# Seven scale-and-shift operations by VectorE instead of ScalarE, in three norms, and a new order of issue

## The chip, the cores and the metric

The kernel runs on one core of one Trainium2 chip. A core has TensorE (PE, matmuls into PSUM), VectorE (DVE), ScalarE (ACT), GpSimd (POOL) and SyncE (SP, which issues nearly all transfers). Each engine takes its own instructions strictly in the order in which they were written for it, and waits at an instruction until what it needs is there. The metric is device microseconds (us) of one execution; of several runs the median counts.

## The reference

One transformer block over a sequence of 2048 rows of width 512, conditioned on a vector `c`:

```
mod = silu(c) @ w_mod                      # six vectors: sa, ca, ga, sb, cb, gb
h = layernorm(x) * (1 + ca) + sa           # first norm, scale and shift
x = x + ga * (attention(h) @ wo)           # 32 heads of 16, each row sees 8 rows, 2 apart
h = layernorm(x) * (1 + cb) + sb           # second norm, scale and shift
x = x + gb * ((gelu(h @ w_gate) * (h @ w_up)) @ w_down)     # width 1792
```

The scale `1 + ca` and shift `sa` are one number for each of the 512 columns. After the norm the tile is transposed, so that a column lies in one partition; scale and shift are then one instruction on 128 partitions with a scalar for each partition.

## The kernel before

The sequence is cut into four groups (0 to 3; the "third group" is group 2) of 512 rows. Each group passes through the same steps:

- first norm `LN1.g`: statistics and normalizing on VectorE and ScalarE, one power on GpSimd, a transposition by DMA (`LN1.g.t`; for groups 0 and 1 by TensorE), and four scale-and-shift operations, one for each 128 columns (`h0` to `h3`, `transp_ev`, lines 511 to 530);
- twelve projections `qp.g.blk.j` (query, key, value; line 632), each four matmuls into one of four PSUM buffers called `mm`, emptied by ScalarE (lines 648 to 652);
- attention: products of query and key by VectorE (`pq`, line 710), their sums over a head by TensorE (`LTp`, line 727), the softmax (maximum, difference, exponential on ScalarE at line 755, sum, reciprocal, product at lines 744 to 775), a round trip of the weights through DRAM (lines 802 and 809), products with the values by VectorE (`pv`, lines 821 and 886), sums by TensorE (lines 837 and 907), emptied by ScalarE into `oT` (lines 848 and 920), output projection (line 930), and its sum with `x` by VectorE (line 939);
- second norm `LN2.g`, as the first; for group 0 in two halves of 256 rows (`half_ev`, lines 957 to 974), which makes eight scale-and-shift operations of half the size;
- the feed-forward part: 14 pairs of gate and up projections (`g`, `u`, line 991; the first two pairs of group 0 in halves, line 1004), gelu and a cast on ScalarE (lines 1038 and 1045), their product on VectorE (`hht`, line 1056), and four down projections (`y`, line 1018), added to `x` on VectorE (line 1063) and stored.

What stands behind what on each engine is set by the table `ORDER` at the top of the file. Every step is a thread of operations (`Op`), and `ORDER` lists 923 thread numbers: `Issuer.run` takes the next operation of that thread and writes its instructions. An operation also names what it takes and gives back (a PSUM buffer, a tile); the table's order decides which buffer it gets and whom it must wait for. So attention of later groups runs between feed-forward matmuls of earlier ones.

Which engine does a scale-and-shift operation is set by two constants: `DVE_H` (line 489, by norm: which of `h0` to `h3` go to VectorE; empty before) and `HALF_DVE` (line 955, for group 0's second norm: pairs of half and column block). The two engines do the same arithmetic with other instructions:

```
nc.vector.tensor_scalar(out=o, in0=o, scalar1=sc(dt), scalar2=bi(dt), op0=ALU.mult, op1=ALU.add)
nc.scalar.activation(out=o, in_=..., func=ACT.Identity, scale=sc(dt), bias=bi(dt))
```

Of the kernel before, what the change touches and what calls it, by code (L numbers as in the profile page):

```python
# [15 lines left out]
NEG = -4.0e9  # L16

ORDER = [
# [37 lines left out]
]  # L56


# [49 lines left out]
def kernel(  # L108
# [377 lines left out]

    PART = ((0, (0, 1), False), (0, (2, 3), True), (1, (0,), False), (1, (1, 2, 3), True))

    DVE_H = {}

    BY_PE = ("LN1.1",)

# [14 lines left out]
    def transp_ev(key, dkey, dtag, sc, bi, ev, dep, eng=False):  # L507
        pe = ev in BY_PE
        for dtp in range(2):
            for dd in range(2):  # L510
                dt = 2 * dtp + dd

                onv = dt in DVE_H.get(ev, ())
                if onv != eng:
# [437 lines left out]
            yield Op("SP", 0.9, f, after=[f"LN2.0.x{2 * h + 1}"], take=[] if h else [SL["h2"]], give=[SL["xn"]] if h else [],  # L952
                     fire=f"LN2.0.th{h}", lat=0.6)

    HALF_DVE = ((1, 2), (1, 3))

    def half_ev(eng):
        for h in range(2):
            for dt in range(DT):
                if ((h, dt) in HALF_DVE) != eng:  # L960
                    continue
# [188 lines left out]
```

## Time and profile before

| | |
|---|---|
| median of 3 runs | 237.56 us (235.99 to 239.63) |
| the profiled execution | 236.0 us, of which the span from first to last instruction is 234.3 us |
| VectorE busy | 183.6 us (78%), 262 instructions |
| ScalarE busy | 148.7 us (63%), 279 instructions |
| GpSimd busy | 16.2 us (7%) |
| granted TensorE clock | 1.00 over the whole span |
| read from and written to HBM | 21.47 MB and 5.57 MB |

How to read the profile's rows. In the timeline a row is: start in us, length in us, engine, line, operation, output <- input, shapes, and the number of instructions merged into it; in brackets how long the engine had idled before, and who released it. Instructions of one engine overlap a little (the next starts before the last one's write-back has ended), so the time that one costs in a row of equal ones is the distance between starts. This matters most for TensorE, whose single matmul is shown with 0.38 us although the next starts 0.216 us later. In the table by stretches, a row is: stretch in us, its length, and for each engine the busy time and instructions, then granted clock, DMA share and GB/s. In the chain of waits a row is start, length, engine, what.

### The profile page before, as it was taken

What the parts mean: (1) busy time and instruction counts of PE and PEld (TensorE: products, weight loads), DVE (VectorE), ACT (ScalarE), POOL (GpSimd) and SP (SyncE); (2) the same over time, 40 slices, a digit from 0 to 9 for tenths busy, and PEclk for the clock granted to TensorE, in tenths of its full rate; (3) what the DMA queues carried; (4) which work ended last, traced back from release to release, by engine and by line L of the source; (5) the groups of instructions that cost most, each with busy time, mean ns of one, the idle gap of its engine ahead of it and who ended that gap; (6) DMA issues with size and microseconds to landing.
All of it is one profiled execution on the core that took longest, in us unless ns stands there. A gap on an engine that the chain in (4) does not pass through costs nothing.

```text
span 234.3 us, 3756 instructions
## 1 busy us (share of the span) xinstructions
PE 228.3 (97%) x1408; PEld 111.2 (47%) x1408; DVE 183.6 (78%) x262; ACT 148.7 (63%) x279; POOL 16.2 (7%) x38
## 2 busy tenths in 40 slices
PE   7999999999989999999999999999999999999995
PEld 2897444454554434444444344444444444444443
DVE  4699989999999999999999698999996831222222
ACT  6699997697897557955769544463764126666400
POOL 3212320121200000010000001000000100000000
PEclk9999999999999999999999999999999999999999
DMA  6998779939658795016700223131111060000021
GB/s 221 358 351 233 222 233 296 277 118 375 135 155 275 217 345 187 1 46 162 223 3 1 61 65 60 30 90 45 25 46 67 0 134 25 0 0 0 3 67 45
DMA packets 37769, 30.43 MB, mean 130 GB/s; under 512 B 22520, under 2 KB 34296, under 8 KB 37752
## 3 DMA queue, kind: packets, MB, share of 16 engines
q1 hardware_dynamic: 37216, 29.68, 43.3%
q10 hardware_dynamic: 536, 0.53, 0.6%
q8 instruction: 11, 0.18, 0.3%
q14 instruction: 6, 0.05, 0.1%
HBM read 21.47 MB, written 5.57 MB: 115 GB/s over the span
## 4 chain that ended last, share of the span: by engine, by line
PE 79%; ACT 14%; DMA 5%; ACTq 0%; issue 0%; SPq 0%; DVE 0%
PE g_ps L991 20%; PE u_ps L991 20%; PE y_ps L1018 19%; PE qkv_ps L632 7%; PE x_ps L930 6%; DMA x<-in_A_x_dram 3%; PE LTp L727 3%; ACT hT L524 2%; DMA wm<-in_w_mod_dram 2%; PE o_ps L907 2%; ACT gl L412 2%; ACT gl L406 1%; PE y_ps L1029 1%; ACT h L969 1%; ACT kT L650 1%; ACT qT L648 1%
## 5 line engine op out<-in xcount | busy, mean ns | idle before, releaser
L991 PE MATMUL g_ps<-h,Wg 128*128 128x512 bf16 x216 | 55.5, 379 | 0.1
L991 PE MATMUL u_ps<-h,Wu 128*128 128x512 bf16 x216 | 55.4, 379 | 0.0
L1038 ACT ACTIVATE gl<-g_ps 128x512 bf16<-128x512 f32 x56 | 33.8, 604 | 21.0 <-PE g_ps L991 19.9
L1018 PE MATMUL y_ps<-Wd,hht 128*128 128x512 bf16 x210 | 46.1, 379 | 0.0
L1045 ACT CAST ub<-u_ps 128x512 bf16<-128x512 f32 x56 | 33.0, 589 | 18.9 <-PE u_ps L991 18.9
L1056 DVE TENSOR_TENSOR hht<-gl,ub 128x512 bf16<-128x512 bf16 x56 | 22.8, 417 | 21.7 <-ACT ub L1045 21.6
L710 DVE TENSOR_TENSOR pq<-qT,kT 128x4096 bf16<-128x4096 bf16 (+1 forms) x17 | 36.2, 2152 | 0.0
L632 PE MATMUL qkv_ps<-hT,wqkv 128*128 128x512 bf16 x144 | 32.9, 380 | 0.7 <-ACT hT L524 0.6
L991 PEld LDWEIGHTS <-Wg 128*128 128x128 bf16 x216 | 20.9, 98 | 26.3 <-issue 1.9
L991 PEld LDWEIGHTS <-Wu 128*128 128x128 bf16 x216 | 20.8, 98 | 26.3 <-issue 1.3
L1018 PEld LDWEIGHTS <-hht 128*128 128x128 bf16 x210 | 20.5, 98 | 24.8
L632 PEld LDWEIGHTS <-wqkv 128*128 128x128 bf16 x144 | 15.8, 114 | 16.7 <-issue 3.6
L1063 DVE TENSOR_TENSOR ot<-y_ps,x 128x512 bf16<-128x512 f32 x15 | 10.2, 686 | 13.0 <-PE y_ps L1018 13.0
L454 POOL TENSOR_TENSOR rstd<-rstd,neghalf 128x4 f32<-128x4 f32 (+1 forms) x10 | 9.3, 932 | 149.3 <-DVE rstd L443 81.7
L524 ACT ACTIVATE h<-h,modT,scl 128x512 bf16<-128x512 bf16 x12 | 8.8, 803 | 16.9 <-DMA h<-xn 11.9
L886 DVE TENSOR_TENSOR pv<-PT,V 128x4096 bf16<-128x4096 bf16 x8 | 18.1, 2282 | 0.4 <-PE LTp L727 0.4
L930 PE MATMUL x_ps<-woP,oT 128*128 128x512 bf16 x64 | 15.5, 380 | 0.3 <-ACT oT L920 0.2
L423 DVE BATCH_NORM_STATS2 st<-x 128x6 f32<-128x512 bf16 x19 | 12.4, 675 | 2.5 <-DMA x<-in_A_x_dram 2.5
L939 DVE TENSOR_TENSOR x<-x_ps,x 128x512 bf16<-128x512 f32 x16 | 10.7, 680 | 2.7 <-PE x_ps L930 2.6
L571 PE MATMUL qkv_ps<-hT,wqkv 128*128 128x256 bf16 x96 | 11.3, 273 | 0.0
L571 PEld LDWEIGHTS <-wqkv 128*128 128x128 bf16 x96 | 10.3, 113 | 0.7 <-issue 0.6
L930 PEld LDWEIGHTS <-oT 128*128 128x128 bf16 x64 | 6.0, 98 | 8.3 <-ACT oT L920 1.0
(97 smaller groups left out, 234.8 us busy)
## 6 DMA issues: line engine op xcount, KB each, us to landing
V<-vscr SPq DMA_DIRECT2D x12, 526.0 KB, 5.4
wm<-in_w_mod_dram SPq DMA_DIRECT2D x4, 512.0 KB, 7.5
out_dram<-ot SPq DMA_DIRECT2D x15, 128.0 KB, 1.9
Wg<-in_B_w_gate_dram SPq DMA_DIRECT2D x4, 448.0 KB, 4.7
Wu<-in_B_w_up_dram SPq DMA_DIRECT2D x4, 448.0 KB, 6.8
vscr<-vT SPq DMA_DIRECT2D x3, 528.0 KB, 4.5
x<-in_A_x_dram SPq DMA_DIRECT2D x3, 512.0 KB, 8.7
Wd<-in_B_w_down_dram SPq DMA_DIRECT2D x3, 512.0 KB, 6.2
```

Source lines behind the costliest of these rows:

```text
L423: nc.vector.bn_stats(out=k["st", c4][:], in_=src()[:, c4, :])
L524: nc.scalar.activation(out=o, in_=B[key, dtp][:, :, dd, :] if pe else o, func=ACT.Identity, scale=sc(dt), bias=bi(dt))
L571: nc.tensor.matmul(B["qu", h, blk, u][:, jj, :], lhsT=wqkv[blk][:, dt, 2 * u + jj::4], rhs=B["hT", 0][:, 2 * h:2 * h + 2, dt, :], start=st ...
L632: nc.tensor.matmul(ps[:], lhsT=wqkv[blk][:, dt, j::4], rhs=B["hT", sg][:, :, dt, :], start=(dt == 0), stop=(dt == DT - 1))
L710: nc.vector.tensor_tensor(out=B["pq", sg, j][:, :, c0:c1], in0=_ap(B["qT", sg][:, j, c0:c1], [[0, W], [1, c1 - c0]]), in1=_ap(kT[:, j, sg ...
L886: nc.vector.tensor_tensor(out=t[:], in0=_ap(B["PT", sg][:, 0, :], [[SG, 2], [0, 4], [1, SG]]), in1=_ap(v[:, j, 0, :], [[8, 2], [VR, 4], [1 ...
L930: nc.tensor.matmul(ps[:], lhsT=B["oT", sg][:, j, c4 * P:(c4 + 1) * P], rhs=woP[:, j, :], start=(j == 0), stop=(j == 3))
L991: nc.tensor.matmul(ps[:], lhsT=Wt[:, dt, ft * P:(ft + 1) * P], rhs=B["h2T", sg][:, :, dt, :], start=(dt == 0), stop=(dt == DT - 1))
L1018: nc.tensor.matmul(ps[:], lhsT=B["hh", sg, ft][:, c4 * P:(c4 + 1) * P], rhs=B["Wd", ft // 4][:, ft % 4, :], start=(ft == 0), stop=(ft == F ...
L1038: nc.scalar.activation(out=gl[:], in_=B["g", sg, ft][:], func=ACT.Gelu_apprx_tanh)
L1045: nc.scalar.copy(out=ub[:], in_=B["u", sg, ft][:])
L1056: nc.vector.tensor_tensor(out=hh[:], in0=B["gl", sg, ft][:], in1=B["ub", sg, ft][:], op=ALU.mult)
```

## The change

It does three things.

1. `DVE_H` gives `h1` and `h3` of the third group's first norm and of group 3's second norm to VectorE, two of four each.
2. `HALF_DVE` gives VectorE, of group 0's second norm, five of eight: blocks 2 and 3 of the first half and 1, 2 and 3 of the second. Two of them it had before.
3. `ORDER` is another list of the same length.

No operation is added or removed: ScalarE has seven fewer, VectorE seven more, and TensorE, GpSimd and SyncE have the same ones in another order.

```
-    0, 29, 29, 29, 2, 3, 39, 39, 39, 40, 39, 0, 1, 29, 1, 29, 29, 29, 29, 17, 17, 29, 29, 29, 29, 45, 29, 18, 29,
+    29, 29, 29, 29, 0, 2, 39, 39, 39, 1, 39, 29, 29, 29, 29, 29, 3, 1, 39, 40, 17, 17, 40, 17, 37, 40, 0, 45, 29,
...
-    DVE_H = {}
+    DVE_H = {"LN1.2": (1, 3), "LN2.3": (1, 3)}
...
-    HALF_DVE = ((1, 2), (1, 3))
+    HALF_DVE = ((0, 2), (0, 3), (1, 1), (1, 2), (1, 3))
```

The places on which the prediction rests, in the program's own order. In these rows a name ends in a buffer number; the numbers differ between the two programs.

ScalarE at the third group's first norm, before. `L755` is group 0's exponential, `L412` a square with its sum for group 3's norm, `L648` to `L652` empty a projection out of PSUM, `L524` are the scale-and-shift operations:

```order
L652 CAST vO_592<-qkv_ps_621 128x512
L412 ACTIVATE gl_645,sums_568<-x_387,sums_568 128x512
L755 ACTIVATE LTp_455<-LTp_455 128x1024
L652 CAST vO_592<-qkv_ps_650 128x512
L648 CAST qT_594<-qkv_ps_656 128x512
L650 CAST kT_137<-qkv_ps_661 128x512
L648 CAST qT_594<-qkv_ps_666 128x512
L524 ACTIVATE hT_679<-hT_679,modT_128,scl_129 128x4x128 x4
L650 CAST kT_137<-qkv_ps_686 128x512
```

And after:

```order
L652 CAST vO_609<-qkv_ps_629 128x512
L755 ACTIVATE LTp_452<-LTp_452 128x1024
L412 ACTIVATE gl_663,sums_613<-x_552,sums_613 128x512
L648 CAST qT_619<-qkv_ps_643 128x512
L650 CAST kT_137<-qkv_ps_655 128x512
L524 ACTIVATE hT_634<-hT_634,modT_128,scl_129 128x4x128
L648 CAST qT_619<-qkv_ps_695 128x512
L524 ACTIVATE hT_634<-hT_634,modT_128,scl_129 128x4x128
L650 CAST kT_137<-qkv_ps_701 128x512
```

Two of the four `L524` are gone; one emptying that stood ahead of the four now stands between the two that are left, and the exponential has moved ahead of a square and behind one emptying of the value projection.

VectorE at the same place, before. `L760` to `L775` end group 0's softmax, `L463` normalizes rows for group 3's first norm, `L710` are group 1's query-key products, `L821` the first value products of group 0:

```order
L760 TENSOR_REDUCE ssum_675<-LTp_455 128x128
L766 RECIPROCAL rinv_677<-ssum_675 128x128
L463 TENSOR_SCALAR xn_698<-x_387,mv_567,rstd_569 128x512
L775 TENSOR_TENSOR e_712<-LTp_455,rinv_677 128x2x4x128
L463 TENSOR_SCALAR xn_698<-x_387,sums_568,rstd_569 128x512 x2
L710 TENSOR_TENSOR pq_748<-qT_594,kT_137 128x4096
L710 TENSOR_TENSOR pq_777<-qT_594,kT_137 128x4096
L463 TENSOR_SCALAR xn_698<-x_387,sums_568,rstd_569 128x512
L710 TENSOR_TENSOR pq_805<-qT_594,kT_137 128x4096
L821 TENSOR_TENSOR pv_808<-PT_745,V4_714 128x2048 x2
```

And after, where `L522` are the scale-and-shift operations:

```order
L522 TENSOR_SCALAR hT_634<-hT_634,scl_129,modT_128 128x4x128
L766 RECIPROCAL rinv_669<-ssum_665 128x128
L522 TENSOR_SCALAR hT_634<-hT_634,scl_129,modT_128 128x4x128
L775 TENSOR_TENSOR e_674<-LTp_452,rinv_669 128x2x4x128
L710 TENSOR_TENSOR pq_676<-qT_619,kT_137 128x4096
L463 TENSOR_SCALAR xn_689<-x_552,mv_612,rstd_614 128x512
L710 TENSOR_TENSOR pq_746<-qT_619,kT_137 128x4096
L710 TENSOR_TENSOR pq_748<-qT_619,kT_137 128x4096
L463 TENSOR_SCALAR xn_689<-x_552,sums_613,rstd_614 128x512 x3
L821 TENSOR_TENSOR pv_808<-PT_691,V4_678 128x2048 x2
```

Both moved operations stand ahead of `L775`, whose result goes to DRAM and back before `L821` can start; group 3's normalizing now ends behind the third `L710` instead of ahead of it.

VectorE at group 0's second norm, before. `L966` are its scale-and-shift operations, the softmax is group 1's, `L710` are group 2's products:

```order
L710 TENSOR_TENSOR pq_1096<-qT_710,kT_137 128x4096
L760 TENSOR_REDUCE ssum_1098<-LTp_779 128x128
L966 TENSOR_SCALAR h2_1085<-h2_1085,scl_129,modT_128 128x2x128 x2
L766 RECIPROCAL rinv_1124<-ssum_1098 128x128
L775 TENSOR_TENSOR e_1126<-LTp_779,rinv_1124 128x2x4x128
L710 TENSOR_TENSOR pq_1140<-qT_710,kT_137 128x4096
```

And after:

```order
L710 TENSOR_TENSOR pq_1088<-qT_729,kT_137 128x4096
L966 TENSOR_SCALAR h2_1104<-h2_1104,scl_129,modT_128 128x2x128 x2
L760 TENSOR_REDUCE ssum_1119<-LTp_793 128x128
L966 TENSOR_SCALAR h2_1104<-h2_1104,scl_129,modT_128 128x2x128 x3
L766 RECIPROCAL rinv_1126<-ssum_1119 128x128
L775 TENSOR_TENSOR e_1128<-LTp_793,rinv_1126 128x2x4x128
L710 TENSOR_TENSOR pq_1138<-qT_729,kT_137 128x4096
```

The first half's two stand ahead of the sum, the second half's three behind it, all ahead of the reciprocal. Further down, on TensorE, one group of four `u` matmuls (the up projection of block 10 in group 1) that stood behind the first two output projections of group 2 (`L930`, eight matmuls) now stands ahead of them, directly behind the attention sums `L907` from which ScalarE makes their input; and group 2's gate projection of block 13 stands ahead of group 3's first two output projections instead of behind them.

Among the transfers, group 3's input `x3` is issued behind three weight transfers instead of ahead of them, and the transposition `LN1.3.t` stands at the same place of the queue, but waits for normalizing that VectorE now does later.

72 rows, old and new, of the table ORDER are left out of this document.

## Prediction

> **What bounds the kernel now.** I read the page first, then the busy time by stretches, then TensorE's timeline for gaps, then ScalarE's and VectorE's rows beside each gap.
>
> ```profile
> PE 228.3 (97%) x1408; PEld 111.2 (47%) x1408; DVE 183.6 (78%) x262; ACT 148.7 (63%) x279; POOL 16.2 (7%) x38
> 30.00:36.00 6.00, 5.32 (x23) 2.38 (x22) 5.42 (x10) 6.00 (x11) 1.48 (x3) 1.00 0.74 245
> 60.00:66.00 6.00, 5.50 (x28) 2.78 (x27) 6.00 (x12) 5.45 (x11) 1.24 (x3) 1.00 0.63 120
> 72.00:98.00 26.00, 26.00 (x182) 11.25 (x181) 25.30 (x28) 17.39 (x38) 0.00 (x0) 1.00 0.66 214
> 98.00:126.00 28.00, 27.98 (x164) 11.88 (x163) 27.43 (x30) 19.48 (x30) 1.03 (x1) 1.00 0.34 91
> ```
>
> The columns after the length are PE, weight loads, DVE, ACT, POOL. TensorE is full but for a few places, and the busy shares understate the gaps there, because an isolated matmul is shown longer than it costs in a row. VectorE is as full as TensorE up to 126 us: what it takes over has no idle time to fall into.
>
> ```profile
> 183.01 12.09 PE y_ps L1018 x56
> 25.98 8.59 PE L632 MATMUL qkv_ps<-hT,wqkv 128*128 128x512 bf16 x38
> 36.07 7.07 PE qkv_ps L632 x32
> 64.46 0.60 PE L1004 MATMUL g_ps<-h,Wg 128*128 128x256 bf16 x2
> 69.62 1.02 PE L991 MATMUL g_ps<-h,Wg 128*128 128x512 bf16 x4
> 131.87 1.05 PE L907 MATMUL o_ps<-pv,Mph 128*32 128x512 bf16 x16
> 132.85 0.61 PE L930 MATMUL x_ps<-woP,oT 128*128 128x512 bf16 x2
> 135.19 1.03 PE L991 MATMUL u_ps<-h,Wu 128*128 128x512 bf16 x4
> ```
>
> The rate is 12.09 / 56 = 0.216 us for a matmul of 512 columns, so 0.865 for a group of four. *Gap A:* nine groups of group 1's projections start at 25.98 and could be done at 25.98 + 36 x 0.216 = 33.76, group 2's first at 34.62; its second starts at 36.07, 1.45 late. *Gap B:* 32 half-size matmuls (0.108 each, 3.46) lie between 64.46 and 69.62, which is 5.16: 1.70 lost. *Gap C:* eight output projections (1.73) take from 132.85 to 135.19: 0.61 lost. All three together are 3.8 us. No edit of this kind can bring more.
>
> ```profile
> 28.90 0.86 ACT L412 ACTIVATE gl<-x,sums 128x512 bf16<-128x512 bf16 x1
> 29.61 1.15 ACT L755 ACTIVATE LTp<-LTp 128x1024 f32<-128x1024 f32 x1
> 31.98 0.75 ACT L648 CAST qT<-qkv_ps 128x512 bf16<-128x512 f32 x1
> 32.46 3.08 ACT L524 ACTIVATE hT<-hT,modT,scl 128x512 bf16<-128x512 bf16 x4
> 35.30 0.72 ACT L650 CAST kT<-qkv_ps 128x512 bf16<-128x512 f32 x1
> 63.65 2.07 ACT L969 ACTIVATE h<-h,modT,scl 128x256 bf16<-128x256 bf16 x4
> 66.57 1.09 ACT L969 ACTIVATE h<-h,modT,scl 128x256 bf16<-128x256 bf16 x2
> 67.68 1.28 ACT L1038 ACT_TABLE_LOAD   x1
> 132.97 1.07 ACT L920 CAST oT<-o_ps 128x512 bf16<-128x512 f32 x2 [2.89 <-PE o_ps L907]
> ```
>
> Gap A ends with the four scale-and-shift operations and the emptying behind them, gap B with ScalarE's six, the table load and the first gelu, gap C with the emptying of the attention sums. ScalarE ends every gap.
>
> **The change part by part.**
>
> *Third group's first norm.* One operation costs ScalarE (35.30 - 32.46) / 4 = 0.71, one emptying 32.46 - 31.98 = 0.48. With one emptying moved behind `h0`, ScalarE starts `h0` at 31.98, then empties until 33.17, does `h2` until 33.88, and has emptied the buffer that group 2's second projection waits for at 34.36. TensorE is ready at 34.62. Gap A closes: a lead of 1.45, if VectorE's two come in time.
>
> ```profile
> 25.24 0.73 DVE L463 TENSOR_SCALAR xn<-x,mv,rstd 128x512 bf16<-128x512 bf16 x2
> 25.89 0.40 DVE L463 TENSOR_SCALAR xn<-x,sums,rstd 128x512 bf16<-128x512 bf16 x1
> 30.79 1.22 DVE L760 TENSOR_REDUCE ssum<-LTp 128x128 f32<-128x1024 f32 x1 [0.51 <-ACT LTp L755]
> 34.28 0.73 DVE L463 TENSOR_SCALAR xn<-x,sums,rstd 128x512 bf16<-128x512 bf16 x2
> 34.39 0.33 SPq L802 DMA_DIRECT2D escr<-e  x1
> 42.27 4.63 DVE L821 TENSOR_TENSOR pv<-PT,V 128x2048 bf16<-128x2048 bf16 x4 [0.34 <-DMA PT<-escr]
> 62.25 2.28 DVE L710 TENSOR_TENSOR pq<-qT,kT 128x4096 bf16<-128x4096 bf16 x1
> 64.45 1.21 DVE L760 TENSOR_REDUCE ssum<-LTp 128x128 f32<-128x1024 f32 x1
> 65.58 0.59 DVE L966 TENSOR_SCALAR h<-h,scl,modT 128x256 bf16<-128x256 bf16 x2
> 66.09 0.94 DVE L766 RECIPROCAL rinv<-ssum 128x128 f32<-128x128 f32 x1
> 68.21 2.28 DVE L710 TENSOR_TENSOR pq<-qT,kT 128x4096 bf16<-128x4096 bf16 x1
> 128.95 2.28 DVE L886 TENSOR_TENSOR pv<-PT,V 128x4096 bf16<-128x4096 bf16 x1
> ```
>
> The new full-size operation has no row. Nearest is `L463`, same engine operation and shape: (25.89 - 25.24) / 2 = 0.33. The tile is strided in blocks of 128, as `L966`'s is, whose half costs (66.09 - 65.58) / 2 = 0.26; twice that, 0.51, is the upper end. I take 0.33, since `L966` pays a start for each half. What it delays: the exponential comes 0.71 - 0.48 = 0.23 earlier (a square behind it, an emptying ahead), one normalizing of 0.33 leaves, two operations of 0.33 enter, a short `rstd` of 0.1 moves ahead. The weights are done 34.28 - 0.23 - 0.33 + 0.66 + 0.1 = 34.48 to, without the overlap that the moved normalizing had, 34.6: 0.2 to 0.3 later, and with them the store at 34.39. VectorE waited 0.34 for their return before 42.27. Its queue fills that: three products of 64.45 - 62.25 = 2.20 and four normalizings from 34.55 on give 42.5. So the value products start at 42.55, 0.3 late by either road. The lead of 1.45 is mostly gone there: TensorE waits for these products and for the scaling of `wo` behind them, and 0.3 late on VectorE means TensorE can keep only what it had spare.
>
> *Group 0's second norm.* From 42 to 66 VectorE has no idle time and the same instructions in another order, so the products at 62.25 start at 62.55 and end at 64.75. Two halves at 0.26 end at 65.27, the sum (65.58 - 64.45 = 1.13) at 66.40, three halves at 67.18. ScalarE starts its first at 64.0 (its forerunner, the exponential, follows VectorE's 0.3), does two of 0.50 each, two emptyings, the third at 66.45, and then the table load: 67.7 instead of 68.96. The first gelu empties its buffer at 68.3. TensorE's last input, `h3`, comes at 67.2, and after it three half groups of 0.43 remain: 68.6. So the row at 69.62 comes at about 68.7: lead 0.9. Gap B shrinks from 1.7 to about 0.8, now ended by VectorE.
>
> *VectorE behind it.* The products at 68.21 start at 68.21 + 0.3 + 3 x 0.26 = 69.3, 1.1 late. Between 72 and 126 VectorE idles 0.70 + 0.57 = 1.27, all of it waiting for others; late, it waits less. So the last value product of group 2, at 128.95, starts between 128.8 (all absorbed) and 130.05 (none) and ends 2.2 later, at 131.0 to 132.25. TensorE comes to these sums at 131.87 - 0.9 = 130.97, to the second eight of them at 131.4. I take near full absorption, because the waits in question are short and at TensorE's pace.
>
> *Gap C.* An up-projection group of 0.865 now stands between the attention sums and the output projection, while ScalarE's two emptyings (1.07) run; the last of them is needed only by the fourth matmul, 0.65 later still. Gain 0.6. This cover holds as long as the last product is on time; else TensorE waits at the sums.
>
> *At no price:* group 3's second norm. The old operations run inside 12.09 us of down projections:
>
> ```profile
> 191.60 2.93 ACT L524 ACTIVATE h<-h,modT,scl 128x512 bf16<-128x512 bf16 x4 [7.92 <-DMA h<-xn]
> 48.59 2.94 ACT L524 ACTIVATE hT<-hT,modT,scl 128x512 bf16<-128x512 bf16 x4
> 39.80 3.71 SPq L483 DMA_TRANSPOSE hT<-xn  x1
> hT<-xn SPq DMA_TRANSPOSE x2, 4.3
> ```
>
> They end at 194.53, before 195.10. Two on VectorE end earlier, but the output projection moved 0.865 closer uses that up; were the cover gone, each microsecond would cost one. `x3`, later by three transfers, is hidden by the work that stands ahead of its first reading on ScalarE. The start (a warm-up matmul moved out of an idle stretch, dummy exponentials elsewhere) I put at 0.1 lost, bounds 0 to 0.3, from one matmul of 0.216 and a short activation.
>
> [...] The row says 0.33 for the moved operation. [...]
>
> **Sum.** Lead 0.9, gap C 0.6, start -0.1: 1.4 us off the profiled execution's 236.0, so 234.6. The median shown is 1.56 above that execution; with the same distance, 236.2.
>
> **The rivals.**
>
> *VectorE keeps it all.* Nothing of its lag is absorbed: the last product ends at 132.25, TensorE's lead there falls from 0.9 to 0.1 (its second eight started at 132.36), gap C still closes: gain 0.6, 237.0. For it: 25.30 of 26.00 busy. Against it: the idle time is there.
>
> *GpSimd blocks the moved operations.* In the new order the power for group 3's norm is released directly ahead of `h1`.
>
> ```profile
> 5.97 1.52 POOL L454 TENSOR_TENSOR rstd<-rstd,neghalf 128x2 f32<-128x2 f32 x2 [3.32 <-DVE mv L429]
> 6.72 0.73 DVE L463 TENSOR_SCALAR xn<-x,mv,rstd 128x512 bf16<-128x512 bf16 x2
> ```
>
> If it held VectorE for its 0.76, everything from 42.55 on would be later by that: gain 0.5 to 0.6, 237.0. The row against it: beside the second power VectorE's two took 0.73, as at 25.24. [...]
>
> *Slower: the transposition for group 3.* Its rows are now normalized at 42.5, not 39.7, so it is issued 2.8 later. ScalarE wants it at about 48.05, half a microsecond before the old 48.59, since the emptyings ahead of it come that much earlier. Landing in 4.3 leaves 1.2. Beyond 5.5 after issue TensorE waits one for one, since the whole of group 3's projections queue behind; at 6.9 the gain is gone, at 8 it is 1 us slower, 238.7. For it: its issue alone took 3.71 in this crowded stretch. Against: both landed in 4.3.
>
> *More.* If the weights return early and VectorE is not late at all, up to 1 us more of the lead survives: 235.2; all three gaps closed would be 233.8.
>
> **Chances.** Forecast 0.52, VectorE keeps it 0.2, GpSimd 0.05, transposition 0.1, more 0.08, unnamed 0.05. The range 233.8 to 238.7 runs from all gaps closed to the transposition's case. A measurement can tell about 2% (4.75 us) from no change; no case but an unnamed one reaches that: faster 0.04, within 0.91, slower 0.05.
>
> **What would show it.** Step one: no gap around 34 to 36 us, and the chain there without `L524`. Step two: `L821` starts at 42.3 to 42.8 and TensorE waits before the first `L930`. Step three: full-size `g` matmuls at 68.7, VectorE's products at 69.3. Step four: no idle before the second `L930` group near 132. VectorE rows of line 522 well over 0.4, `L821` after 43.5, or `L524` waiting for a transfer near 48 would make it wrong.

## The result and the profile after

The changed kernel takes 235.5 us (median of 20 runs, 234.33 to 238.77), the one before 237.59 (20 runs beside it). The ratio is 0.9918, with a 95% interval of 0.9891 to 0.9945: 0.8% faster, 1.95 us, which is less than the 2% that count as a difference here. The ratio and its interval are formed from the fast executions alone, the medians from all. The forecast was 236.2, in a range of 233.8 to 238.7. The profiled execution took 234.34 us, its span is 232.5.

The page's busy line and the table by stretches of the changed kernel, with the columns as before:

```profile
PE 226.4 (97%) x1397; PEld 111.3 (48%) x1408; DVE 185.1 (80%) x269; ACT 144.6 (62%) x272; POOL 18.2 (8%) x38
...
30.00:36.00 6.00, 6.00 (x30) 3.13 (x28) 5.57 (x9) 5.40 (x11) 1.46 (x3) 1.00 0.82 262
60.00:66.00 6.00, 5.77 (x33) 3.21 (x31) 6.00 (x12) 5.52 (x12) 1.12 (x3) 1.00 0.59 120
72.00:98.00 26.00, 25.95 (x181) 11.11 (x180) 26.00 (x29) 18.01 (x40) 0.00 (x0) 1.00 0.57 171
98.00:126.00 28.00, 27.93 (x164) 12.16 (x164) 27.72 (x31) 19.41 (x29) 1.03 (x1) 1.00 0.39 110
```

Between 30 and 36 us TensorE went from 5.32 to 6.00 of 6.00: gap A is gone. VectorE went from 25.30 to 26.00 in 72 to 98 and from 27.43 to 27.72 in 98 to 126: of its 1.27 us of idle time in these stretches 0.99 is gone. TensorE's rows at the three gaps (a row's count can be one short, where a matmul's record is missing):

```profile
26.18 17.47 PE L632 MATMUL qkv_ps<-hT,wqkv 128*128 128x512 bf16 x80
...
48.21 1.89 PE L930 MATMUL x_ps<-woP,oT 128*128 128x512 bf16 x7 [0.73 <-ACT kT L650]
...
64.39 0.27 PE L1004 MATMUL g_ps<-h,Wg 128*128 128x256 bf16 x1
...
64.88 0.52 PE L1004 MATMUL g_ps<-h,Wg 128*128 128x256 bf16 x3 [0.22 <-ACT h L969]
...
68.44 1.03 PE L991 MATMUL g_ps<-h,Wg 128*128 128x512 bf16 x4
...
130.62 1.05 PE L907 MATMUL o_ps<-pv,Mph 128*32 128x512 bf16 x16
131.60 1.04 PE L991 MATMUL u_ps<-h,Wu 128*128 128x512 bf16 x4
132.47 1.89 PE L930 MATMUL x_ps<-woP,oT 128*128 128x512 bf16 x7
...
226.40 3.22 PE L1029 MATMUL y_ps<-Wd,hht 128*128 128x384 bf16 x28
```

Eighty projection matmuls now run in one row from 26.18. The 32 half-size matmuls take 68.44 - 64.39 = 4.05 for 3.46, so 0.59 is lost where it was 1.70, and behind the attention sums of 130.62 the `u` group fills the time until the output projection can start. VectorE and ScalarE beside them:

```profile
31.91 0.41 DVE L522 TENSOR_SCALAR hT<-hT,scl,modT 128x512 bf16<-128x512 bf16 x1
32.08 1.10 POOL L454 TENSOR_TENSOR rstd<-rstd,neghalf 128x4 f32<-128x4 f32 x1 [1.66 <-DVE rstd L448]
32.23 0.95 DVE L766 RECIPROCAL rinv<-ssum 128x128 f32<-128x128 f32 x1
33.09 0.31 DVE L522 TENSOR_SCALAR hT<-hT,scl,modT 128x512 bf16<-128x512 bf16 x1
33.32 1.22 DVE L775 TENSOR_TENSOR e<-LTp,rinv 128x1024 bf16<-128x1024 f32 x1
34.46 2.28 DVE L710 TENSOR_TENSOR pq<-qT,kT 128x4096 bf16<-128x4096 bf16 x1
...
42.35 4.62 DVE L821 TENSOR_TENSOR pv<-PT,V 128x2048 bf16<-128x2048 bf16 x4
...
46.89 1.22 DVE L389 TENSOR_TENSOR woP<-woP,gB 128x2048 bf16<-128x2048 bf16 x1
...
48.35 2.96 ACT L524 ACTIVATE hT<-hT,modT,scl 128x512 bf16<-128x512 bf16 x4
...
62.27 2.28 DVE L710 TENSOR_TENSOR pq<-qT,kT 128x4096 bf16<-128x4096 bf16 x1
...
66.31 1.28 ACT L1038 ACT_TABLE_LOAD   x1
...
69.01 2.28 DVE L710 TENSOR_TENSOR pq<-qT,kT 128x4096 bf16<-128x4096 bf16 x1
...
128.11 2.28 DVE L886 TENSOR_TENSOR pv<-PT,V 128x4096 bf16<-128x4096 bf16 x1
```

The first moved operation costs VectorE 32.23 - 31.91 = 0.32, with a power on GpSimd (`L454`) beside it, the second 33.32 - 33.09 = 0.23. The value products did not wait for the weights this time. What ends last has moved as well. In the chain of waits, the kernel before first, then the changed one, VectorE had no share before and has 23% now:

```profile
PE 79%; ACT 14%; DMA 5%; ACTq 0%; issue 0%; SPq 0%; DVE 0%
```

```profile
PE 59%; DVE 23%; ACT 13%; issue 3%; DVEq 0%
```

**How the traces are compared.** The first 26 us hold the loads (the DMA share is 0.92 there in the changed kernel), and one execution of the same start is up to 1.3 us later there than another: the row of projections near 26 us began at 26.16 to 27.49 in the eleven traces whose start is that of the new order, at 25.98, 26.33 and 27.11 in the three with the old (means 26.86 and 26.47). So below, every start is counted from that row, and the "end" is the start of the last down projections (line 1029). By this the gain is 202.19 - 200.22 = 1.97 us, which agrees with the ratio of the times. The 0.1 us that the forecast put on the start cannot be seen under that spread. Each kernel has one trace, so a distance also holds the waits that this one execution happened to have; two such waits are told below.

| kernel | first output projection | full-size g | group 0's down proj. | group 1's | group 2's | end | ratio of times, 95% |
|---|---|---|---|---|---|---|---|
| before | 22.64 | 43.64 | 72.15 | 116.98 | 156.87 | 202.19 | 1 |
| changed | 22.03 | 42.26 | 70.92 | 114.93 | 154.89 | 200.22 | 0.9918 (0.9891 to 0.9945) |
| order_alone | 22.98 | 44.48 | 73.14 | 117.14 | 157.11 | 202.44 | 1.0029 (1.0002 to 1.0057) |
| engines_alone | 22.66 | 43.85 | 72.36 | 117.18 | 157.07 | 203.44 | 1.0049 (1.0021 to 1.0078) |
| no_ln12 | 22.98 | 43.25 | 71.91 | 115.91 | 155.88 | 201.20 | 0.9960 (0.9927 to 0.9993) |
| no_ln20 | 22.02 | 43.51 | 72.16 | 116.17 | 156.13 | 201.46 | 0.9981 (0.9947 to 1.0015) |
| no_ln23 | 22.03 | 43.16 | 71.82 | 115.82 | 155.79 | 201.11 | 0.9925 (0.9895 to 0.9955) |
| ln23_late | 22.41 | 42.65 | 71.31 | 115.31 | 155.28 | 201.65 | 0.9956 (0.9929 to 0.9983) |
| gapc_undone | 22.42 | 43.55 | 72.21 | 117.04 | 157.00 | 202.33 | 0.9961 (0.9934 to 0.9988) |
| gapc_alone | 22.70 | 44.65 | 73.16 | 117.54 | 157.52 | 202.85 | 1.0002 (0.9979 to 1.0025) |
| double_pv | 23.84 | 44.08 | 72.74 | 116.74 | 156.71 | 202.03 | 0.9969 (0.9936 to 1.0002) |
| mod4x4 | 22.50 | 43.62 | 72.28 | 116.29 | 156.25 | 201.57 | 0.9979 (0.9951 to 1.0007) |
| mod_early | 22.03 | 42.27 | 70.93 | 114.94 | 154.90 | 200.23 | 0.9927 (0.9902 to 0.9952) |
| tuned | 21.98 | 42.26 | 70.92 | 114.92 | 154.89 | 200.21 | 0.9936 (0.9904 to 0.9968) |

The lead grows at three places: 0.61 at the first output projection, 1.38 at full-size `g` (1.23 at group 0's down projections), 2.05 at group 1's.

### The profile page after: what moved, and what is told of

It is laid out like the page before. It is cut to its first block, busy times and chain, and to the rows that moved or that the text cites. A ratio compares the mean times of both kernels' runs of the same rounds, so it can differ in the third digit from the quotient of the medians.

```text
span 232.5 us, 3744 instructions
## 1 busy us (share of the span) xinstructions
PE 226.4 (97%) x1397; PEld 111.3 (48%) x1408; DVE 185.1 (80%) x269; ACT 144.6 (62%) x272; POOL 18.2 (8%) x38
## 4 chain that ended last, share of the span: by engine, by line
PE 59%; DVE 23%; ACT 13%; issue 3%; DVEq 0%
PE y_ps L1018 18%; PE u_ps L991 16%; PE g_ps L991 16%; DVE pq L710 8%; DVE pv L821 3%; DVE pv L886 3%; PE x_ps L930 3%; ACT gl L412 3%; ACT gl L406 2%; PE warm_ps L206 2%; PE y_ps L1029 1%; ACT hT L524 1%; DVE hht L1056 1%; ACT ub L1045 1%; DVE x L939 1%
## 5 line engine op out<-in xcount | busy, mean ns | idle before, releaser
L710 DVE TENSOR_TENSOR pq<-qT,kT 128x4096 bf16<-128x4096 bf16 (+1 forms) x17 | 36.3, 2155 | 0.0
L632 PE MATMUL qkv_ps<-hT,wqkv 128*128 128x512 bf16 x144 | 32.2, 380 | 0.0
L524 ACT ACTIVATE h<-h,modT,scl 128x512 bf16<-128x512 bf16 x10 | 7.4, 804 | 22.1 <-DMA h<-xn 22.1
L454 POOL TENSOR_TENSOR rstd<-rstd,neghalf 128x4 f32<-128x4 f32 (+1 forms) x10 | 9.4, 941 | 140.3 <-DVE rstd L443 85.0
L930 PE MATMUL x_ps<-woP,oT 128*128 128x512 bf16 x59 | 14.7, 379 | 1.0 <-ACT kT L650 0.7
L930 PEld LDWEIGHTS <-oT 128*128 128x128 bf16 x64 | 6.2, 98 | 8.4 <-ACT kT L650 1.0
```

The lines of the kernel that those rows point to most:

```text
L632: nc.tensor.matmul(ps[:], lhsT=wqkv[blk][:, dt, j::4], rhs=B["hT", sg][:, :, dt, :], start=(dt == 0), stop=(dt == DT - 1))
L710: nc.vector.tensor_tensor(out=B["pq", sg, j][:, :, c0:c1], in0=_ap(B["qT", sg][:, j, c0:c1], [[0, W], [1, c1 - c0]]), in1=_ap(kT[:, j, sg ...
L930: nc.tensor.matmul(ps[:], lhsT=B["oT", sg][:, j, c4 * P:(c4 + 1) * P], rhs=woP[:, j, :], start=(j == 0), stop=(j == 3))
```

## The experiments

**The order and the engines apart.** The first kernel has the new order and all seven operations on ScalarE, the second the old order and the seven on VectorE, in the old places (of group 0's second norm, the three directly ahead of the two that VectorE had). The edit of the first, against the changed kernel:

```
-    DVE_H = {"LN1.2": (1, 3), "LN2.3": (1, 3)}
+    DVE_H = {}
-    HALF_DVE = ((0, 2), (0, 3), (1, 1), (1, 2), (1, 3))
+    HALF_DVE = ((1, 2), (1, 3))
```

> The new order with all seven operations back on ScalarE (each behind its neighbour there). Theory (each closed gap brings its own lead, the order alone closes only gap C): ScalarE does h0 and h1, one emptying, h2 and h3, so group 2's second projection starts near 36.2 instead of without a gap; the first output projection at 48.6 to 48.8 (changed kernel 48.21, before 48.62); full-size g at 69.4 to 69.7 (68.44; 69.62); no idle at 132 to 135; span 233.7 (changed 232.5, before 234.3). Rival (the order carries the whole gain and the engine of the seven does not matter): span 232.3 to 232.7. Rival (the two belong together, neither is worth anything without the other): span 234.3 or more.

> The old order with the seven operations on VectorE, in the old places (the three of group 0's second norm directly ahead of the two that VectorE had, behind the sum). Theory: gap A closes, but VectorE's two of 0.33 delay the value products to 42.9 (before 42.27) and the first output projection to 49.1 (48.62); at group 0's second norm h2 and h3 of the first half come behind the products and the sum, at 66.4 to 66.7, so the half-size matmuls wait there and full-size g starts at 69.6 to 70.2 (69.62); gap C stays; span 234.3 to 235.0. Rival (fewer operations on ScalarE are the gain, wherever VectorE does them): span 233.0.

Neither brings anything: +0.25 us and +1.25 us on the kernel before, both slower by the times, by less than 1%. For the order alone the second rival held. Gap C did close there (117.14 - 73.14 = 44.00, before 44.83), but 1.0 us was lost ahead of it. The engines alone stayed near the kernel before up to group 2's down projections (+0.20), as the theory had it, and then lost 1.05 at a place that I had costed at nothing, group 3's second norm (from those down projections to the end 46.37, before 45.32). VectorE's timeline there, and TensorE's row that waits for it:

```profile
195.69 0.69 DVE L1063 TENSOR_TENSOR ot<-y_ps,x 128x512 bf16<-128x512 f32 x1 [2.33 <-PE y_ps L1018]
196.30 0.73 DVE L522 TENSOR_SCALAR h<-h,scl,modT 128x512 bf16<-128x512 bf16 x2
196.75 0.81 PE L991 MATMUL g_ps<-h,Wg 128*128 128x512 bf16 x3 [0.89 <-DVE h L522]
```

In the old places the two stand behind a sum of VectorE that itself waits for the last down projection, and the feed-forward part waits for them.

**The third group's first norm back on ScalarE.** The new order, `h1` behind `h0` and `h3` behind `h2` on ScalarE.

```
-    DVE_H = {"LN1.2": (1, 3), "LN2.3": (1, 3)}
+    DVE_H = {"LN2.3": (1, 3)}
```

> The changed kernel with the two operations of the third group's first norm back on ScalarE. Theory (TensorE's lead from gap A is mostly lost at the first output projection): a gap of 1.0 to 1.3 us is back at 34 to 36.2, but VectorE's value products start 0.5 to 0.7 earlier and TensorE only loses its 0.73 of waiting ahead of the first output projection, which comes at 48.5 to 48.8 (48.21); full-size g at 68.7 to 69.0; span 232.7 to 233.1. Rival (VectorE alone decides at 48): the first output projection at 47.6 to 48.2, span 232.0 to 232.5. Rival (the closed gap is kept whole): span 233.6.

The end came 0.98 later. That is the number of the rival "kept whole", and not of my theory, that the lead of gap A is mostly lost at the output projection. But it did not come by the rival's road. The value products did start earlier, 15.85 after the row near 26 instead of 16.17, as the theory had it; then something else held VectorE. First TensorE at gap A, then VectorE at the value products:

```profile
36.88 9.28 PE L632 MATMUL qkv_ps<-hT,wqkv 128*128 128x512 bf16 x41 [0.32 <-ACT hT L524]
...
43.22 2.36 DVE L821 TENSOR_TENSOR pv<-PT,V 128x2048 bf16<-128x2048 bf16 x2
...
46.76 2.36 DVE L821 TENSOR_TENSOR pv<-PT,V 128x2048 bf16<-128x2048 bf16 x2 [1.18 <-PE LTp L727]
```

With the gap back, TensorE comes late to the sums of group 1's query-key products (`L727`), which free the product buffers, and VectorE, two operations lighter, stands 1.18 us for them. So at 46 us VectorE depends on TensorE as much as the other way round; `order_alone` has the same wait, with 1.11. The new order has put the first of these sums two projections later (from ahead of `qp.2.1.2` to behind `qp.2.0.3`). That this move makes the wait is read from the rows; it was not tried by itself. The kernel before does not have this wait, so the 0.98 is what the two operations are worth within the new order; against the kernel before, 0.61 of gap A's 1.45 is left at the output projection.

**Group 0's second norm back on ScalarE.**

```
-    HALF_DVE = ((0, 2), (0, 3), (1, 1), (1, 2), (1, 3))
+    HALF_DVE = ((1, 2), (1, 3))
```

> The changed kernel with the three operations of group 0's second norm back on ScalarE (VectorE keeps the two it had before). Theory: ScalarE's table load is at 67.7 (66.31), full-size g at 69.3 to 69.6 (68.44), VectorE's products behind it at 68.2 (69.01); the lead of 0.8 to 1.1 us is gone to the end: span 233.3 to 233.6. Rival (VectorE's lag of 0.8 costs TensorE as much later as it gains here): span 232.3 to 232.7.

Full-size `g` came 1.25 later and the end 1.24: the theory held, at somewhat more than its size. The two parts add up: 0.98 + 1.24 = 2.22, which is what `order_alone` lost on the changed kernel (202.44 - 200.22).

**Group 3's second norm: back on ScalarE, and later on VectorE.** The sequence is that of `ORDER`, in step names (`ot.2.2` and `ot.2.3` are VectorE's last two sums of group 2's down projections, `sto` a store; `ot.2.3` waits for the last down projection). In the second kernel the two operations stand behind both sums, which is two places later in VectorE's queue, not one.

```
-    DVE_H = {"LN1.2": (1, 3), "LN2.3": (1, 3)}
+    DVE_H = {"LN1.2": (1, 3)}
```

```
-    LN2.3.h1, LN2.3.h3, ot.2.2, sto.2.1, ot.2.3,
+    ot.2.2, sto.2.1, ot.2.3, LN2.3.h1, LN2.3.h3,
```

> The changed kernel with the two operations of group 3's second norm back on ScalarE. Theory (hidden behind down projections, as predicted): the four end 0.4 us after the down projections do, but the last is wanted only by the fourth matmul, 0.65 later; distance 200.2 to 200.4. Rival (the output projection that was moved closer used up the cover): g of group 3 starts late or waits, distance 200.6 to 201.0.

> The changed kernel with VectorE's two operations of group 3's second norm one place later in VectorE's queue, behind its last sum of group 2's down projections. Theory (the place in the other engine's queue decides, not the engine): that sum waits for the last down projection, so the two come at 194.0 to 194.7 and TensorE waits for them inside the first gate projection, 0.8 to 1.1 us; distance 201.0 to 201.3. Rival (the gate projections behind have slack in PSUM and the wait is made up): distance 200.2 to 200.5.

Back on ScalarE, the stretch from group 2's down projections to the end is 45.32 (changed 45.33): worth nothing, as predicted. This trace is 0.9 late nonetheless, but from full-size `g` on, for a reason that comes below. Behind the two sums in VectorE's queue, the same stretch is 46.37, 1.04 more: the theory held, and it is all that `engines_alone` lost there.

**Gap C undone, and alone.** Undone: in the changed kernel `u.1.10` goes back behind the output projections `x1p.2.0` and `x1p.2.1`. Alone: the opposite move in the kernel before. The lines show the first (four operations of ScalarE and VectorE stand at the dots; `ub.1.10` is a cast on ScalarE, whose own order stays).

```
-    u.1.10, ..., x1p.2.0, hh.1.9, ub.1.10, x1p.2.1,
+    ..., x1p.2.0, hh.1.9, x1p.2.1, u.1.10, ub.1.10,
```

> The changed kernel with group 1's up projection of block 10 back behind the first two output projections of group 2 (and its cast right behind it). The time is read as a distance within the trace, from the row of projections near 26 us to the last down projections (L1029), since the start before that row differs from one execution to the next: 202.19 before, 200.22 changed. Theory (the group covers the emptying of the attention sums): TensorE waits again inside the first output projections, 0.6 to 0.8 us, distance 200.8 to 201.0. Rival (by now the sums come early enough, TensorE has nothing to wait for): distance 200.1 to 200.4.

> The kernel before with one edit: group 1's up projection of block 10 ahead of the first two output projections of group 2 instead of behind them. No operation changes its engine. Theory (gap C is a matter of the order alone, as large as it was when undone in the changed kernel, 0.82 us from the down projections of group 0 to those of group 1): that stretch 43.9 to 44.1 (44.83 before), end distance 201.3 to 201.5 (202.19), ratio 0.996 to 0.997. Rival (in the old order the attention sums come too late to cover, since VectorE's products end there): stretch 44.5 to 44.9, nothing gained.

From group 0's to group 1's down projections the undone kernel takes 44.83 (changed 44.01): 0.82, the upper end of the expectation. The move alone takes 44.38 (before 44.83): 0.45, between the theory and the rival. In the undone kernel the gap is back, 136.21 - 133.87 = 2.34 for eight output projections as before:

```profile
133.87 0.61 PE L930 MATMUL x_ps<-woP,oT 128*128 128x512 bf16 x2
134.63 1.74 PE L930 MATMUL x_ps<-woP,oT 128*128 128x512 bf16 x6 [0.15 <-ACT oT L920]
136.21 1.03 PE L991 MATMUL u_ps<-h,Wu 128*128 128x512 bf16 x4
```

In the kernel with the move alone it is closed; TensorE has all sixteen output projections in one row:

```profile
134.01 1.05 PE L907 MATMUL o_ps<-pv,Mph 128*32 128x512 bf16 x16
134.99 1.04 PE L991 MATMUL u_ps<-h,Wu 128*128 128x512 bf16 x4
135.86 3.77 PE L930 MATMUL x_ps<-woP,oT 128*128 128x512 bf16 x16
```

Where the other 0.37 lies can be read from the four traces by cutting the stretch at the row of attention sums (`L907`) ahead of the gap. From there to group 1's down projections the kernel before takes 142.96 - 131.87 = 11.09, the changed one 141.11 - 130.62 = 10.49, the move alone 10.64, the undone kernel 11.31. So gap C itself is worth 0.60 in the changed kernel. The move alone loses 0.15 of that within its sixteen output projections, and the undone kernel loses 0.22 more than the kernel before, at its second eight. Ahead of the sums the stretch takes 33.74 before and with the move alone, 33.52 in the changed and in the undone kernel: this 0.22 has nothing to do with gap C. The only thing in TensorE's order there that differs is where the sums of group 3's query-key products stand: in two rows before, in one in the new order, here the kernel before, then the changed one:

```profile
110.31 1.05 PE L727 MATMUL LTp<-pq,Mph 128*32 128x512 bf16 x16
...
116.58 1.05 PE L727 MATMUL LTp<-pq,Mph 128*32 128x512 bf16 x16
```

```profile
112.73 1.91 PE L727 MATMUL LTp<-pq,Mph 128*32 128x512 bf16 x32
```

The times of the move alone (1.0002) show no gain, but they could not exclude 0.45 us, which is 0.9981; its trace ends 0.66 later than the kernel before's, because it lost 1.01 ahead of the stretch, to the wait that comes and goes (below).

**What VectorE's lateness costs.** In the changed kernel the first value product is made twice (the lines behind 821 have one number more in this trace).

```
+                    for _ in range(2 if (h, j) == (0, 0) else 1):
```

> The changed kernel with VectorE's first value product of group 0 (line 821) made twice, 1.15 us more on VectorE at 42 us, to measure what VectorE's lateness costs there. Theory (VectorE and TensorE arrive together at the second eight of group 0's attention sums, so lateness passes on whole and VectorE, without idle time until 126 us, does not make it up): first output projection 1.0 to 1.15 later counted from the row near 26 us (22.03 changed), distance 201.1 to 201.4. Rival (TensorE's 0.73 of waiting ahead of the output projection swallows most): 0.3 to 0.5 later, distance 200.5 to 200.8.

Everything came 1.81 later, from the first output projection to the end, more than expected. VectorE's rows and TensorE's say where it comes from:

```profile
42.94 5.89 DVE L822 TENSOR_TENSOR pv<-PT,V 128x2048 bf16<-128x2048 bf16 x5 [0.46 <-DMA gB<-gscr]
...
48.75 1.22 DVE L389 TENSOR_TENSOR woP<-woP,gB 128x2048 bf16<-128x2048 bf16 x1
...
48.88 0.40 PE L838 MATMUL o_ps<-pv,Mph 128*32 128x256 bf16 x8 [0.73 <-DVE pv L822]
...
50.06 1.89 PE L931 MATMUL x_ps<-woP,oT 128*128 128x512 bf16 x8 [0.78 <-ACT oT L849]
```

The products began 0.55 later than in the changed kernel's trace (16.72 instead of 16.17 after the row near 26), because VectorE waited for a transfer, and the five took 48.75 - 42.94 = 5.81 until the scaling of `wo`. Four took 46.89 - 42.35 = 4.54 in the changed kernel, so the fifth cost 1.27. Together that is 1.82. Lateness here passes on whole to the end: TensorE's 0.73 of waiting swallows none of it, and VectorE makes up none. `ln23_late`, whose value products began 0.37 late for the same kind of wait, says it without an added product: 0.38 late at the output projection, 0.39 at group 2's down projections.

**A wait that comes and goes.** Two traces with the new order, `no_ln23` and `gapc_undone`, lost 0.9 between the first output projection and full-size `g`, where the same instructions stand as in the changed kernel. GpSimd's rows there, of the changed kernel and then of `no_ln23`:

```profile
61.66 0.41 POOL L329 TENSOR_SCALAR scl<-modc 128x4 f32<-128x4 bf16 x1 [0.30 <-DMA modc<-gscr]
```

```profile
63.02 2.39 POOL L329 TENSOR_SCALAR scl<-modc 128x4 f32<-128x4 bf16 x1 [0.90 <-DMA modc<-gscr]
65.37 0.18 POOL L327 CAST modT<-modc 128x4 f32<-128x4 bf16 x1
65.58 1.09 ACT L969 ACTIVATE h<-h,modT,scl 128x256 bf16<-128x256 bf16 x2 [0.98 <-POOL modT L327]
```

A scale of four numbers for each partition took 2.39 us instead of 0.41, when its transfer landed just as VectorE's long product began (63.02 and 63.03). In `gapc_undone` its row even starts 0.27 ahead of the product's (63.37 and 63.64), and it took 2.64. One kernel makes the scale four times, so that the last one falls beside the product also when the transfer lands early; another starts the chain of the scale earlier (`gc4`, an emptying by ScalarE).

```
-  ... lambda: nc.gpsimd.tensor_scalar_add(out=scl[:, 4:8], in0=modc[:, 4:8], scalar1=1.0)
+  ... lambda: [nc.gpsimd.tensor_scalar_add(out=scl[:, 4:8], in0=modc[:, 4:8], scalar1=1.0) for _ in range(4)]
```

```
-    LN1.3.h3, qp.3.0.0, qkv.3.0.0, gc4,
+    LN1.3.h3, gc4, qp.3.0.0, qkv.3.0.0,
```

> The changed kernel with GpSimd's small scale of the second norm (line 329, 128x4) made four times instead of once, at 61.7 us, directly ahead of VectorE's products that start near 62.3. In two of the eight traces with the new order this operation took 2.4 to 2.6 us instead of 0.23 to 0.45, where it started beside those products, and group 0's second norm waited for it. Theory (GpSimd is held while a product of VectorE runs, and the new order leaves the scale only just ahead of it): one of the four takes 2 us or more, the scale-and-shift operations of group 0's second norm wait for GpSimd until 65 or later, full-size g comes 0.8 to 1.0 later than the 42.26 us after the row near 26. Rival (it was the late transfer, not VectorE): four take 0.2 to 0.4 each, all is done before 63.7, where ScalarE wants it, and g stays at 42.2 to 42.7.

> The changed kernel with one small emptying on ScalarE (line 377, from which the scale of the second norm comes through DRAM) one place earlier, ahead of group 3's first projection. Theory: the chain to GpSimd's scale is 0.8 to 1.0 earlier, the scale is done before VectorE's products start and takes 0.2 to 0.45; full-size g at 42.2 to 42.7 after the row near 26, end distance 200.2 to 200.6; the median gains only as often as the wait came, 0 to 0.5 us on the changed kernel's, ratio 0.989 to 0.992. Rival (the landing of its transfer is set by the weights in the same queues, not by when it is issued): the scale is no earlier, and the wait comes as before in some executions.

For the four scales the theory held. GpSimd's and VectorE's rows with four scales, and the group of the four (shortest, median and longest in ns):

```profile
62.07 3.30 POOL L329 TENSOR_SCALAR scl<-modc 128x4 f32<-128x4 bf16 x4
62.99 2.29 DVE L710 TENSOR_TENSOR pq<-qT,kT 128x4096 bf16<-128x4096 bf16 x1
65.32 0.18 POOL L327 CAST modT<-modc 128x4 f32<-128x4 bf16 x1
```

```profile
L329 POOL TENSOR_SCALAR scl<-modc x4: 222/226/2380, 62.1 to 63.0; 128x4 f32<-128x4 bf16 x4
```

Three take 0.22 to 0.23, and the one that meets VectorE's product takes 2.38, until that product ends. Full-size `g` came 1.36 later: 0.47 is the first output projection's lateness (VectorE waited for a transfer ahead of the value products, as in `double_pv`), the other 0.89 is the wait. With the earlier emptying (25.01 after the row near 26 instead of 26.16) the scale waited for no transfer and took 0.23, `g` came at 42.27 and the end at 200.23, as the theory had it. But of the eight traces with the new order and the old place of the emptying six went without the wait too, so one trace does not show that the edit removes it, and its ratio, 0.9927, cannot be told from the changed kernel's. The old order knows the wait too: in `gapc_alone` GpSimd's cast took 1.62 beside the same products, and full-size `g` came 1.01 later than before.

**A try for more.** On top of the earlier `gc4`, two emptyings of key projections on ScalarE are moved out from between the two emptyings of the attention sums. The lines show ScalarE's operations alone.

```
-    oTh.0.0, qkv.2.1.3, gc3, qkv.1.1.3, oTh.0.1,
+    qkv.1.1.3, qkv.2.1.3, oTh.0.0, gc3, oTh.0.1,
```

> As the kernel with the earlier emptying of line 377, and besides two emptyings of key projections on ScalarE (line 650) moved out from between the two emptyings of group 0's attention sums (line 848) into the 2 us that ScalarE waits ahead of the first. Theory: the second emptying of the sums ends 0.5 earlier, and the first output projection waits for VectorE's scaling of wo alone: it starts 5.6 to 5.8 us after the first value product instead of 5.86; end distance 199.9 to 200.4, ratio 0.988 to 0.991. Rival (VectorE's scaling ends last already): 5.8 to 5.9, nothing gained. Nearer than 0.3 us the times cannot tell; the trace decides.

The rival held: the first output projection came 5.82 after the first value product (changed 5.86), and the end at 200.21. VectorE and TensorE in this trace:

```profile
48.20 1.22 DVE L389 TENSOR_TENSOR woP<-woP,gB 128x2048 bf16<-128x2048 bf16 x1
...
49.47 1.89 PE L930 MATMUL x_ps<-woP,oT 128*128 128x512 bf16 x8 [0.68 <-ACT oT L848]
```

The scaling of `wo` ends at 49.42, just ahead of 49.47. By the times, none of the kernels tried can be told to be faster than the changed one.

## Why the prediction was right, step by step

*Gap A, and VectorE's lateness behind it.* The gap closed as put. The price of a moved operation was put at 0.33 and measured 0.32 and 0.23. The step that was mis-sized is "So the value products start at 42.55, 0.3 late by either road": on the clock of the row near 26 that is 16.57, and the trace has 16.17 (before 16.29). One of its two roads, VectorE's queue, was 0.35 too long, and 0.29 of that lies ahead of the weights, which were put 0.2 to 0.3 late and were not late at all. Their last product in the kernel before is

```profile
33.15 1.22 DVE L775 TENSOR_TENSOR e<-LTp,rinv 128x1024 bf16<-128x1024 f32 x1
```

7.17 after the row near 26, and 7.14 in the changed one (33.32). From the start of the sum (`L760`) to this product VectorE took 2.62 instead of 2.36, where 0.43 more were put, and the sum started 0.29 earlier on that clock, where 0.23 were put. So 0.61 of the lead was left at the output projection, where I had it mostly gone. The other road, the return of the weights through DRAM, is real, though: in `ln23_late` VectorE waited 0.29 for it. In `gapc_undone`, `mod4x4` and `double_pv` it waited 0.29 to 0.46 at the same place for a transfer (`gB<-gscr`, as the rows name it). In these four the products began at 16.54 to 16.72, and in all but `double_pv` the output projection came at 22.41 to 22.50; so there the lead left is 0.14 to 0.23. In the profiled execution, and in four others with these two operations on VectorE, there was no such wait; that the profiled one is among them is luck. What the step left out is the other direction: `no_ln12` shows that VectorE needs TensorE's lead for its product buffers.

*Gap B.* Forecast: full-size `g` at 68.7, 0.9 earlier; ScalarE's table load done at 67.7; VectorE's products behind at 69.3. On the clock of the kernel before (0.20 taken off, the distance between the two rows near 26) they came at 68.24, 67.39 and 68.81: `g` 1.38 earlier, all 0.3 to 0.5 ahead of the forecast. The difference is VectorE's lateness that did not come: its products put at 62.55 started at 62.07 on that clock, 0.48 ahead of the forecast, and 0.40 of that was there at the value products. The mechanism (ScalarE out, VectorE in) holds, and undoing it costs 1.25.

*VectorE's lag absorbed.* The last value product of group 2 was put at 128.8 if all is absorbed; it came at 128.11, 1.04 us earlier than before counted from the row near 26. Of the lead only 0.15 was lost between `g` and group 0's down projections. The rival "VectorE keeps it all" is out.

*Gap C.* Forecast 0.6, measured 0.60 from the attention sums on: right in place and size. The stretch that holds it gained 0.82, because the sums of group 3's query-key products stand in one row instead of two, 0.22. That 0.22 is in none of the three gaps, so "No edit of this kind can bring more" than these was too narrow. The move alone brings 0.45; the rest depends on the order around it.

*At no price.* Right for the change as made, and shown by `no_ln23`: there the four on ScalarE end at 195.31, 0.49 behind the start of the first gate projection, and nothing waits. But the reason given ("Two on VectorE end earlier") was not the one that matters. It is their place in VectorE's queue: behind the next two sums they cost 1.04.

*The other rivals.* GpSimd did not block the moved operations: VectorE's cost 0.32 beside a power on GpSimd (line 454, 1.10 from 32.08). The transposition for group 3 came in time: the four `L524` at 48.35 waited for nothing.

*Sum.* 0.61, 0.77 more at gap B, 0.15 lost behind it, 0.82 from group 0's to group 1's down projections (0.60 of it gap C), 0.08 lost behind that: 1.97 on the clock of the row near 26, against 0.9 + 0.6 = 1.5 put. The profiled execution took 234.34 against 234.6 put. The median, 235.5 against 236.2, is off by 0.7, of which 0.4 is the distance between the median and the profiled execution: it was taken over as 1.56, without a reason, and was 1.16.

## What to carry to other kernels

Moving an operation to another engine is two decisions, the engine and the place in that engine's queue, and here neither was worth anything without the other: the engines alone cost 1.25 us, the order alone 0.25, both together gained 1.97. Before costing a moved operation at nothing, look at the instruction that would stand ahead of it in the new queue, and at what that one waits for: here two places made 1.04 us. And where one execution differs from the next by as much as the effect, count from a row behind the scattered part, and look for waits that some traces have and others lack.

## What the runs showed of the hardware

Small GpSimd operations that ran beside VectorE's long products lasted until the product ended: in `mod4x4` the scale of line 329, 0.22 us alone, took 2.38, and VectorE's product beside it took 2.29, where the next one, with no GpSimd operation beside it, took 2.28. The changed kernel's trace has it too: GpSimd's copies of lines 666 and 659, 0.24 us each at 29.89 and 30.18, took 1.83 at 23.66, 1.47 at 40.09 and 2.44 at 50.91, and ended each time 0.1 behind a product, twice of line 710 and the last time of line 821. What holds GpSimd there no run shows. I had weighed this only as a danger to VectorE, where no row shows it (a moved operation cost 0.32 beside a power on GpSimd); it hit small GpSimd operations, and it turned the lateness of one transfer into a wait of 0.9 us that came in some executions only. Rows of one engine overlap: the operation of line 522 at 33.09 is 0.31 long, and the next starts at 33.32, 0.08 before its end; the traces show the overlap and not its cause. Up to the row near 26 us the fourteen profiled executions lie 1.5 us apart, more than most of the effects measured here.
